# Attention and Fourier mixing on one core: late v chains and imaginary-row chains run as pairs on 64 rows each, with the score maxima in the same TensorE mode

## The chip, the cores and the metric

The kernel runs on one core of a Trainium2 chip. The metric is the device time of one execution in microseconds, the median of several runs; lower is better. Before the change it is 1739.28 us (three runs, 1739.17 to 1740.05).

## The reference, cut to what matters

```python
# S = 2048 rows, D = 512, H = 32 heads of 16
g = sigmoid((x * gate_w).sum(-1, keepdims=True))
# A: Fourier mixing, real part only
a = x @ dft_hid_re.T ;  b = x @ dft_hid_im.T
A = dft_seq_re @ a - dft_seq_im @ b
# B: softmax attention of all heads, scale 16 ** -0.5
q, k, v = split(x @ wqkv)
B = softmax(q @ k.T * scale) @ v @ wo
return g * A + (1 - g) * B
```

Everything is float32. The kernel keeps the precision by splitting an operand into a high and a low part (fp32r) and taking three products, high by high, high by low and low by high.

## The kernel before, in words

The work has three stages, one after the other on TensorE (PE).

**Stage 1** (lines 127 to 188) makes q and k from x and writes their high and low parts to DRAM.

**Stage 2** (lines 272 to 310) is the one that the change rewrites. It has 16 tiles of v (`for s in range(NT)`, line 272), then 16 tiles of imaginary rows b (line 296). A tile is a chain of 12 matmuls on all 128 rows of the array (four slices `kt` of 128 by three products, `mm3`, lines 78 to 81; rows here are those of the contraction) into one PSUM bank of pool `psS`. After the chain comes `visit` (line 260). From the eighth v tile on, until 44 units are made (`LEAD`), a visit makes two units ahead of time. A unit is a 128x512 block of scores for both heads of a pair: for each head one matmul on 48 rows (`a_tile`, line 217; head 0 in rows 0 to 47, head 1 in rows 64 to 111) and a DVE reduction that keeps only the row maxima (line 219). So 22 of the 32 visits hold four score matmuls each: three into pool `psA` (3 banks), the last into `psD` (1 bank). Behind the visit the chain's bank is emptied. A v tile takes an ACT copy and a DVE copy of half a bank (lines 280 and 281). A b tile takes `hi_lo` (line 74): an ACT cast to the high part, a DVE subtraction that waits for it, and a 512 KB store on SP's queue (line 305), through a buffer `hl` of which there are two. When a half of the 64 units of a pair is complete, `deferred` gets two steps (`m_parts`, `m_rows`) which reduce the maxima further and write them as rows behind q.

**Stage 3** (lines 770 to 824) holds the attention and the Fourier matmuls together. First come six pumps of real-row matmuls on 128 rows, then segments. A segment (line 744) follows a pattern of slots: `s` is a score matmul on 50 rows with an exponential on ACT behind it (lines 635 and 636), `a` a score matmul for a maximum, `|` the product of the exponentials with v (`pv`, line 644) for one unit. A slot of one letter also issues one matmul of a running chain, on 64 rows of the half of the array that the score does not use (line 349), so that the two stand side by side. Two segments make a pair of segments: in the second the chains move to the other half of the rows, and the scores too. At each such swap the first chain matmul waits for the last user (ACT or DVE) of the segment before (line 760), so that what the old half wrote into the chain's bank is there. Patterns: `THIN` with real-row chains of 12 (13 pairs of segments; each pair holds one whole chain, which its first segment begins), `FULL` with sequence chains of 48 (96 pairs, a chain begins in every third), `NINE` with projection chains of 9 (13 pairs).

PSUM has 8 banks: `psS` 3, `psA` 3, `psD` 1 and `acc` 1. The bank `acc` collects the `pv` products; it is filled with zeros once at the beginning (line 155), since the products write 17 of each 32 rows and all are copied out.

Of the kernel before, what the change touches and what calls it, by code (L numbers as in the profile page):

```python
# [9 lines left out]
F32 = mybir.dt.float32  # L10
# [5 lines left out]
P = 128  # L16
S = 2048
D = 512
# [13 lines left out]
def mix_kernel(ctx: ExitStack, tc: tile.TileContext, xa_t, xa, wqkv, w_hid, w_seq, wo, gate_w, out):  # L32
# [41 lines left out]
    def hi_lo(hi, lo, src, lo_eng=None):  # L74
        nc.scalar.copy(hi, src)  # L75
        (lo_eng or nc.vector).tensor_tensor(lo, src, hi.bitcast(F32), ALU.subtract)

    def mm3(ps, sh, sl, mh, ml, first, last):
        nc.tensor.matmul(ps, sh, mh, start=first, stop=False)  # L79
        nc.tensor.matmul(ps, sh, ml, start=False, stop=False)  # L80
        nc.tensor.matmul(ps, sl, mh, start=False, stop=last)  # L81
# [11 lines left out]
    def staged(src):  # L93
        raw = st1.tile([P, D], F32, name="raw", bufs=RAW)
        nc.sync.dma_start(raw, src)
        return raw
# [30 lines left out]
    with tc.tile_pool(name="qk", bufs=1, reuse_waits="tile") as pool:  # L127
        wh = pool.tile([P, 2, KT, D], F32R, name="wh")
        wl = pool.tile([P, 2, KT, D], F32R, name="wl")

        def mm_qk(ps, c, ct, tb, kt):
            cols = slice(ct * P, (ct + 1) * P)
            x = xab[tb][:, :, :, kt * P:(kt + 1) * P]
            mm3(ps, wh[:, c, kt, cols], wl[:, c, kt, cols], x[:, :, 0], x[:, :, 1], kt == 0, kt == KT - 1)

        def evac_qk(ps, c, ct, tb):
            hl = pool.tile([P, 2, D], F32R, name="hl", bufs=7)
            hi_lo(hl[:, 0], hl[:, 1], ps)
            nc.sync.dma_start(qk_d[c][:, ct * P:(ct + 1) * P, tb * 512:(tb + 1) * 512].rearrange("v p t -> p v t"),
                              hl.bitcast(F32))  # L140

        for kt in range(KT):
            add(wh[:, 0, kt], wl[:, 0, kt], wqkv[0, :, kt], nc.vector)
            add_x(0, kt)
        for kt in range(KT):
            add(wh[:, 1, kt], wl[:, 1, kt], wqkv[1, :, kt], nc.vector)
        for tb in range(1, 4):
            for kt in range(KT):
                add_x(tb, kt)
        for kt in range(KT):  # L150
            add(wv[0][kt], wv[1][kt], wqkv[2, :, kt], nc.gpsimd)
        for kt in range(KT):
            add(wch[:, kt], wcl[:, kt], w_hid[1, :, kt], nc.gpsimd)
        split(8)
        nc.vector.memset(acc, 0.0)

        xgs = {}

        def gate_row(s):

            xg = xgs.pop(s)
            nc.vector.scalar_tensor_tensor(xg, xg, 1.0, gwb, op0=ALU.mult, op1=ALU.mult, accum_out=z[:, s:s + 1])
            if s + 5 < NT:
                xgs[s + 5] = staged(xa[s + 5])

        for tb in range(4):
            if tb == 2:
                assert not todo and not loaded
                nc.sync.dma_start(gwb, gate_w.broadcast_to([P, D]))
                xgs.update({s: staged(xa[s]) for s in range(5)})  # L170
            for c in range(2):
                if tb == 0 and c == 0:
                    pss = [bank() for _ in range(4)]
                    for kt in range(KT):
                        for ct in range(4):
                            mm_qk(pss[ct], c, ct, tb, kt)
                    split(4)
                    for ct in range(4):
                        evac_qk(pss[ct], c, ct, tb)
                    continue  # L180
                for ct in range(4):
                    ps = bank()
                    for kt in range(KT):
                        mm_qk(ps, c, ct, tb, kt)
                    split(1 if ct % 2 and tb else 2)
                    evac_qk(ps, c, ct, tb)
                    if tb > 1:
                        gate_row(8 * (tb - 2) + 4 * c + ct)
# [22 lines left out]
    def a_tile(i, h, ps=None):  # L211
        p, j = divmod(i, 64)
        qt, kb = divmod(j, 4)
        if ps is None:
            ps = psA.tile([P, 512], F32, name="a")
        r = slice(64 * h, 64 * h + 48)
        nc.tensor.matmul(ps, qs[p % 2][r, qt * P:(qt + 1) * P], ks[p % 2][r, kb * 512:(kb + 1) * 512],  # L217
                         start=True, stop=True)
        user = nc.vector.tensor_reduce(mx[p % 2][:, h, qt, kb:kb + 1], ps, AX.X, ALU.max)  # L219
        hf = j // 32  # L220
        a_left[p, hf] = a_left.get((p, hf), 64) - 1
        if not a_left[p, hf]:
            deferred.extend((partial(m_parts, p, hf), partial(m_rows, p, hf)))
        return user
# [18 lines left out]
    def run_deferred():  # L243
        while deferred:
            deferred.pop(0)()


    ones = st1.tile([2, 2 * D], F32, name="hl", bufs=2)
    nc.gpsimd.memset(ones, 1.0)
    nc.gpsimd.memset(vt[:, :, :, 16:17], 1.0)  # L250
    for i in range(2):
# [5 lines left out]
    wrs = []  # L257
    a_next = 0

    def visit(i):  # L260

        nonlocal a_next
        if deferred:
            deferred.pop(0)()
        if i < 7 or a_next == LEAD:
            return
        for j in range(2):
            for h in range(2):
                a_tile(a_next, h, psD.tile([P, 512], F32, name="d") if j and h else None)
            a_next += 1  # L270

    for s in range(NT):
        t = xab[s // 4][:, s % 4]
        ps = psS.tile([P, 512], F32, name="s")
        for kt in range(KT):
            r = slice(kt * P, (kt + 1) * P)
            mm3(ps, t[:, 0, r], t[:, 1, r], wv[0][kt], wv[1][kt], kt == 0, kt == KT - 1)
        visit(s)
        pv = ps.rearrange("p (r h d) -> p r h d", h=2, d=DH)
        nc.scalar.copy(vt[:, s, :, 0:16], pv[:, :, 0])  # L280
        nc.vector.tensor_copy(vt[:, s, :, 17:33], pv[:, :, 1])
        if s in range(6, 14, 2):
            kt = (s - 6) // 2
            wt = st1.tile([P, 2, D], F32R, name="hl", bufs=2)
            hi_lo(wt[:, 0], wt[:, 1], wos.pop(0), nc.gpsimd)
            nc.sync.dma_start(wo_d[kt], wt.bitcast(F32))
            wrs.append(staged(w_hid[0, :, kt]))

    def spare(i, dt, name):

# [2 lines left out]

    wre = [[const.tile([P, D], F32R, name=f"wre{v}{kt}", tag=f"w{4 * v + kt}") for kt in range(KT)] for v in range(2)]
    ab = [xab[s // 4][:, s % 4] for s in range(NT)]
    for s in range(NT):
        t = ab[s]
        ps = psS.tile([P, 512], F32, name="s")
        for kt in range(KT):
            r = slice(kt * P, (kt + 1) * P)  # L300
            mm3(ps, t[:, 0, r], t[:, 1, r], wch[:, kt], wcl[:, kt], kt == 0, kt == KT - 1)
        visit(NT + s)
        bt = st1.tile([P, 2, D], F32R, name="hl", bufs=2)
        hi_lo(bt[:, 0], bt[:, 1], ps)
        nc.sync.dma_start(b_d[s], bt.bitcast(F32))
        if s < KT:
            hi_lo(wre[0][s], wre[1][s], wrs.pop(0), nc.gpsimd)
    run_deferred()
    assert a_next == LEAD
    right.__exit__(None, None, None)  # L310

# [139 lines left out]

    def inverse(hf, ct, n=4):
        rc = rcs.pop((hf, ct))
        for h in range(2):
            rows = rc[64 * h:64 * h + 16 * n]
            nc.vector.reciprocal(rows, rows)
            nc.sync.dma_start(r_d[hf][ct][h, :n].rearrange("p (c f) -> c p f", f=64), rows)

    def load_o(o, sm, hf, ct, q0, n=4):
# [205 lines left out]
    def issue(x, half, stop=True):  # L665
        chain, st, mv, after, last = x
        i = chain.mm(st, mv, half, last and stop)
        if stop and after:
            after()
        return i  # L670
# [73 lines left out]
    def segment(pattern, half, ds, stop):  # L744


        nonlocal users
        before, users = users, []
        ds = iter(ds)
        for slot in pattern.split():  # L750
            if slot == "|":
                values()
                continue
            if len(slot) == 1:
                x = next(ds, None)
                if x:
                    i = issue(x, half, stop)
                    users = []
                    if before:
                        tc.add_manual_dep(  # L760
                            i.ins, dict(before).get("s", before[0][1]).ins.name,
                            mybir.DependencyInfo(mybir.DependencyClass.Sync, mybir.DependencyReason.DATA))
                        before = None
            score(slot[0], 1 - half)
            if len(slot) == 2:
                score(slot[1].lower(), half)
        if deferred:
            deferred.pop(0)()
# [92 lines left out]
```

## Time and profile before

| | |
|---|---|
| median of 3 runs | 1739.28 us |
| profiled execution: its time, its span | 1738.59 us, 1736.8 us |
| granted TensorE clock, mean | 0.998 |
| stage 2: first maximum (line 217) to the first matmul of stage 3 (line 349) | 116.22 to 201.82 us |
| THIN segments | up to about 372 us |
| FULL segments | 374 to about 1516 us |
| NINE segments and the rest | from 1518 us |

The profile gives for each engine the busy time and for each group of instructions the count, the mean duration and what ended the idle time before it. In the timeline a row is a start, a duration, an engine and an operation; `PE` is a matmul, `PEld` a weight load. Matmuls are pipelined, so a row's duration is longer than the step from one matmul to the next: the steps are read from the starts. A PE that is shown as busy all the time can therefore still lose time between matmuls.

### The profile page before, as it was taken

The page shows a single profiled execution, that of the slowest core. Times are in us where ns is not written, and L with a number is a line of the kernel's source. Part 1 is how long each engine was busy: PE and PEld are TensorE (multiplying, and loading weights), DVE is VectorE, ACT ScalarE, POOL GpSimd, SP SyncE. Part 2 cuts the span into 40 slices and gives each one's busy share as a digit, 9 for nine tenths or more (in the row PEclk, how much of TensorE's full clock was granted, in tenths as well). Part 3 has the DMA queues.
Part 4 walks back from the last instruction along what each step waited for, and adds up shares of the span by engine and source line. Part 5 has one row for each costly group of instructions (what it writes and reads, how often), then busy time and mean ns, then how long its engine had stood idle before and what let it go on. Part 6 is the DMA issues. An engine that isn't in the chain of part 4 may idle for free.

```text
span 1736.8 us, 32902 instructions
## 1 busy us (share of the span) xinstructions
PE 1717.9 (99%) x12721; PEld 1036.8 (60%) x12721; DVE 1368.8 (79%) x2302; ACT 1153.1 (66%) x2257; POOL 447.3 (26%) x561
## 2 busy tenths in 40 slices
PE   8999999999999999999999999999999999999998
PEld 7876644456665666666566666666656666544443
DVE  5448688888888888888888888888888888899953
ACT  5211277776776677677677777767776776777776
POOL 1121122222232233222132343332333343200111
PEclk9999999999999999999999999999999999999999
DMA  9962500314141343414146435223142535460113
GB/s 293 337 153 109 158 2 8 56 31 80 38 87 44 74 113 83 77 44 74 43 90 240 94 105 108 68 64 71 49 82 67 124 93 98 166 153 23 38 28 128
DMA packets 82348, 164.79 MB, mean 95 GB/s; under 512 B 19712, under 2 KB 19968, under 8 KB 78352
## 3 DMA queue, kind: packets, MB, share of 16 engines
q1 hardware_dynamic: 77840, 162.30, 36.5%
q8 instruction: 100, 1.64, 0.4%
q0 software_dynamic: 4352, 0.39, 0.3%
q14 instruction: 56, 0.46, 0.1%
HBM read 107.47 MB, written 54.52 MB: 93 GB/s over the span
## 4 chain that ended last, share of the span: by engine, by line
PE 96%; ACT 2%; DVE 1%; DMA 0%; issue 0%; POOL 0%; DVEq 0%; SPq 0%; ACTq 0%; POOLq 0%
PE d L349 35%; PE acc L644 26%; PE s L635 12%; PE a L217 12%; PE s L79 3%; PE s L80 3%; PE s L81 3%; ACT pt L636 1%; PE a L79 1%; PE a L81 1%; PE a L80 1%; ACT y L365 0%; DVE mx L219 0%; PE a L349 0%; DMA qs<-mt 0%
## 5 line engine op out<-in xcount | busy, mean ns | idle before, releaser
L219 DVE TENSOR_REDUCE mx<-a 128x1 f32<-128x512 f32 x2026 | 1245.2, 683 | 251.3 <-PE a L217 233.0
L636 ACT ACTIVATE pt<-s 128x512 f32<-128x512 f32 x2008 | 1025.4, 620 | 391.8 <-PE s L635 333.2
L217 PE MATMUL a<-ks,qs 48*128 48x512 f32 x2026 | 811.9, 418 | 0.7 <-DVE mx L219 0.7
L635 PE MATMUL s<-qs,ks 50*128 50x512 f32 x2008 | 769.9, 413 | 1.3 <-DMA qs<-mt 0.9
L349 PE MATMUL d<-xab,ch 64*128 64x512 f32 x2016 | 648.4, 396 | 0.0
L644 PE MATMUL acc<-pt,vt 128*17 128x512 f32 x4096 | 500.3, 596 | 0.0
L349 PEld LDWEIGHTS d<-xab,ch 64*128 64x128 f32 x2016 | 366.1, 184 | 126.4 <-DVE mx L219 60.4
L635 PEld LDWEIGHTS s<-qs,ks 50*128 50x128 f32 x2008 | 365.7, 184 | 108.2 <-ACT pt L636 31.0
L217 PEld LDWEIGHTS a<-ks,qs 48*128 48x128 f32 x2026 | 365.9, 185 | 73.5 <-DVE mx L219 42.1
L349 PE MATMUL d<-xab,cl 64*128 64x512 f32 x1008 | 399.4, 396 | 0.0
L349 PEld LDWEIGHTS d<-xab,cl 64*128 64x128 f32 x1008 | 185.5, 184 | 65.2 <-DVE mx L219 40.8
L333 POOL CAST ch<-craw 128x512 fp32r<-128x512 f32 x126 | 77.4, 614 | 555.8 <-PE s L635 176.8
L644 PEld LDWEIGHTS acc<-pt,vt 128*17 128x17 f32 x4096 | 90.2, 96 | 205.8 <-issue 205.8
L334 POOL TENSOR_TENSOR cl<-craw,ch 128x512 fp32r<-128x512 f32 x126 | 162.5, 1290 | 10.2
L240 POOL DMA_DIRECT2D qs<-mt x128 | 72.2, 569 | 159.3 <-DVE mt L236 150.9
L349 PE MATMUL d<-wre,xab 64*128 64x512 f32 (+1 forms) x348 | 94.9, 405 | 2.6 <-ACT pt L636 2.5
L349 PEld LDWEIGHTS d<-wre,xab 64*128 64x128 f32 (+1 forms) x348 | 60.0, 185 | 39.3 <-issue 23.2
L349 PE MATMUL d<-wo_hl,o_hl 64*128 64x512 f32 (+1 forms) x261 | 70.8, 397 | 0.0
L75 ACT CAST hl<-s 128x512 fp32r<-128x512 f32 x32 | 18.8, 587 | 65.0 <-PE s L81 49.4
L349 PEld LDWEIGHTS d<-wo_hl,o_hl 64*128 64x128 f32 (+1 forms) x261 | 47.1, 185 | 16.2 <-issue 11.7
L231 POOL CAST nhl<-nm 128x16 fp32r<-128x16 f32 x32 | 6.3, 197 | 160.7 <-DVE nm L228 160.7
L366 POOL CAST xab<-y 128x512 fp32r<-128x512 f32 x16 | 9.8, 613 | 136.9 <-ACT y L365 108.9
(125 smaller groups left out, 932.7 us busy)
## 6 DMA issues: line engine op xcount, KB each, us to landing
craw<-w_seq SPq DMA_DIRECT2D x128, 256.0 KB
qk<-hl SPq DMA_DIRECT2D x32, 512.0 KB
qs<-qk SPq DMA_DIRECT2D x96, 128.0 KB
ks<-qk SPq DMA_DIRECT2D x96, 128.0 KB
b<-hl SPq DMA_DIRECT2D x16, 512.0 KB
xab<-b SPq DMA_DIRECT2D x16, 512.0 KB
o<-oe SPq DMA_DIRECT2D x62, 128.0 KB
oh<-nh SPq DMA_DIRECT2D x12, 512.0 KB
```

Source lines behind the costliest of these rows:

```text
L79: nc.tensor.matmul(ps, sh, mh, start=first, stop=False)
L80: nc.tensor.matmul(ps, sh, ml, start=False, stop=False)
L81: nc.tensor.matmul(ps, sl, mh, start=False, stop=last)
L217: nc.tensor.matmul(ps, qs[p % 2][r, qt * P:(qt + 1) * P], ks[p % 2][r, kb * 512:(kb + 1) * 512], start=True, stop=True)
L219: user = nc.vector.tensor_reduce(mx[p % 2][:, h, qt, kb:kb + 1], ps, AX.X, ALU.max)
L240: (nc.sync, nc.gpsimd)[h].dma_start(rows.rearrange("v (q b c) -> v b q c", q=8, b=4)[:, b], mt[hf][32 * b + h:32 * b + 32:2])
L333: nc.gpsimd.tensor_copy(h1, raw)
L334: nc.gpsimd.tensor_tensor(l1, raw, h1.bitcast(F32), ALU.subtract)
L349: i = nc.tensor.matmul(self.ps, st[r], mv[r], start=not self.begun, stop=stop)
L635: nc.tensor.matmul(ps, ks[p % 2][rr, kt * P:(kt + 1) * P], qs[p % 2][rr, q0:q0 + 512], start=True, stop=True)
L636: return nc.scalar.activation(pts[u][:, 2 * qb + h], ps, AF.Exp, bias=0.0, scale=DH ** -0.5)
L644: nc.tensor.matmul(acc[32 * j:32 * j + 17], vt[:, kt, p, 16 * h:16 * h + 17], pt[:, j], start=kt == 0, stop=kt == NT - 1)
```

## The change

The loops of stage 2 are written anew. The first eight v tiles stay as they were, without visits. The last eight v tiles and all 16 b tiles go in groups of four, each group as two pairs of tiles. A *phase* issues 12 steps for one pair: in each step one matmul of 64 rows for the first tile and one of the other 64 rows for the second. A group has four phases: pair 0 on one assignment of rows, pair 1 likewise, then pair 0 with the rows swapped, pair 1 swapped. So each chain has 24 half matmuls instead of 12 whole ones. A phase with maxima makes two units, one after step 3 and one after step 9 (phases 1 to 22 of 24); the last of the four scores uses the bank `acc` instead of `psD`, since every group has one chain in `psD` and three in `psS`. The first matmul of a swapped phase waits for the DVE reduction of head 1 of the first unit in the phase before. The banks of a pair are emptied after its second phase, both tiles behind one another. The filling of `acc` moves to the end of stage 2, and `hl` has four buffers instead of two.

In stage 3 two things change. `inverse` takes the reciprocal of both heads' sums in one instruction where all four pairs are there (7 of 8 calls). And a segment whose first chain matmul begins a new chain no longer waits for the segment before.

The diff, cut to its core:

```diff
-        nc.vector.memset(acc, 0.0)
-    ones = st1.tile([2, 2 * D], F32, name="hl", bufs=2)
+    ones = st1.tile([2, 2 * D], F32, name="hl", bufs=4)
-    def visit(i):
-        nonlocal a_next
-        if deferred:
-            deferred.pop(0)()
-        if i < 7 or a_next == LEAD:
-            return
-        for j in range(2):
-            for h in range(2):
-                a_tile(a_next, h, psD.tile([P, 512], F32, name="d") if j and h else None)
-            a_next += 1
+    def x_mm(s, wh, wl):
+        t = xab[s // 4][:, s % 4]
+        for kt in range(KT):
+            h1, l1 = (t[:, v, kt * P:(kt + 1) * P] for v in range(2))
+            yield from ((h1, wh[kt]), (h1, wl[kt]), (l1, wh[kt]))
...
+    made, user = 0, None
+    def phase(pair, half, maxima):
+        nonlocal a_next, user
+        before, user = user, None
+        for j in range(12):
+            for x, (ps, ops, done) in enumerate(pair):
+                st, mv = ops[j]
+                r = slice(64 * (half ^ x), 64 * (half ^ x) + 64)
+                i = nc.tensor.matmul(ps, st[r], mv[r], start=not half and not j, stop=half == 1 and j == 11)
+                if not j and not x and half:
+                    tc.add_manual_dep(i.ins, before.ins.name,
+                                      mybir.DependencyInfo(mybir.DependencyClass.Sync, mybir.DependencyReason.DATA))
+            if maxima and j in (3, 9):
+                for h in range(2):
+                    used = a_tile(a_next, h, acc if h and j == 9 else None)
+                user = user or used
+                a_next += 1
+        if half:
+            for ps, ops, done in pair:
+                done(ps)
+        if deferred:
+            deferred.pop(0)()
+    def pairs_of(tiles, wh, wl, done):
+        nonlocal made
+        tiles = list(tiles)
+        for i in range(0, len(tiles), 4):
+            new = []
+            for s in tiles[i:i + 4]:
+                ps = psD.tile([P, 512], F32, name="d") if s % 4 == 1 else psS.tile([P, 512], F32, name="s")
+                new.append((ps, list(x_mm(s, wh, wl)), partial(done, s)))
+            for half in range(2):
+                for pair in (new[:2], new[2:]):
+                    phase(pair, half, 0 < made and a_next < LEAD)
+                    made += 1
+    for s in range(8):
...
+    pairs_of(range(8, NT), *wv, v_done)
...
+    pairs_of(range(NT), *([w[:, kt] for kt in range(KT)] for w in (wch, wcl)), b_done)
     run_deferred()
+    nc.vector.memset(acc, 0.0)
...
         rc = rcs.pop((hf, ct))
+        if n == 4:
+            nc.vector.reciprocal(rc, rc)
         for h in range(2):
             rows = rc[64 * h:64 * h + 16 * n]
-            nc.vector.reciprocal(rows, rows)
+            if n < 4:
+                nc.vector.reciprocal(rows, rows)
...
                 if x:
+                    before = before if x[0].begun else None
                     i = issue(x, half, stop)
```

`v_done` and `b_done` hold what stood behind the visit before: the two copies of a v tile (with a split of `wo` at tiles 6, 8, 10 and 12), and for a b tile the cast, the subtraction and the store, at the first four b tiles also the split of a slice of the real weights (`wre`, a cast on ACT and a subtraction on POOL).

More of the change, by code (lines that the diff above doesn't have):

```diff
@@ L258, in mix_kernel, with v_done @@
     a_next = 0
-    def visit(i):
-        nonlocal a_next
-        if deferred:
-            deferred.pop(0)()
-        if i < 7 or a_next == LEAD:
-            return
-        for j in range(2):
-            for h in range(2):
-                a_tile(a_next, h, psD.tile([P, 512], F32, name="d") if j and h else None)
-            a_next += 1
-    for s in range(NT):
+    def x_mm(s, wh, wl):
         t = xab[s // 4][:, s % 4]
-        ps = psS.tile([P, 512], F32, name="s")
         for kt in range(KT):
-            r = slice(kt * P, (kt + 1) * P)
-            mm3(ps, t[:, 0, r], t[:, 1, r], wv[0][kt], wv[1][kt], kt == 0, kt == KT - 1)
-        visit(s)
+            h1, l1 = (t[:, v, kt * P:(kt + 1) * P] for v in range(2))
+            yield from ((h1, wh[kt]), (h1, wl[kt]), (l1, wh[kt]))
+    def v_done(s, ps):
         pv = ps.rearrange("p (r h d) -> p r h d", h=2, d=DH)
@@ L283, in mix_kernel @@
             kt = (s - 6) // 2
-            wt = st1.tile([P, 2, D], F32R, name="hl", bufs=2)
+            wt = st1.tile([P, 2, D], F32R, name="hl", bufs=4)
             hi_lo(wt[:, 0], wt[:, 1], wos.pop(0), nc.gpsimd)
@@ L287, in mix_kernel, with b_done @@
             wrs.append(staged(w_hid[0, :, kt]))
+    def b_done(s, ps):
+        bt = st1.tile([P, 2, D], F32R, name="hl", bufs=4)
+        hi_lo(bt[:, 0], bt[:, 1], ps)
+        nc.sync.dma_start(b_d[s], bt.bitcast(F32))
+        if s < KT:
+            hi_lo(wre[0][s], wre[1][s], wrs.pop(0), nc.gpsimd)
+    made, user = 0, None
[33 more added lines that the diff above has]
+    for s in range(8):
+        ps = psS.tile([P, 512], F32, name="s")
+        ops = list(x_mm(s, *wv))
+        for i, (st, mv) in enumerate(ops):
+            nc.tensor.matmul(ps, st, mv, start=not i, stop=i == len(ops) - 1)
+        v_done(s, ps)
+    pairs_of(range(8, NT), *wv, v_done)
     def spare(i, dt, name):
@@ L295, in mix_kernel @@
     ab = [xab[s // 4][:, s % 4] for s in range(NT)]
[L296 to L307, printed above, removed]
+    pairs_of(range(NT), *([w[:, kt] for kt in range(KT)] for w in (wch, wcl)), b_done)
     run_deferred()
+    nc.vector.memset(acc, 0.0)
     assert a_next == LEAD
```

## The prediction

> **What bounds the kernel now.** I read the page first: busy time and the chain of work that ended last.
>
> ```profile
> span 1736.8 us, 32902 instructions
> ...
> PE 1717.9 (99%) x12721; PEld 1036.8 (60%) x12721; DVE 1368.8 (79%) x2302; ACT 1153.1 (66%) x2257; POOL 447.3 (26%) x561
> ...
> PE 96%; ACT 2%; DVE 1%; DMA 0%; issue 0%; POOL 0%; DVEq 0%; SPq 0%; ACTq 0%; POOLq 0%
> ```
>
> PE is the bound: 96% of the chain is PE, and every step that PE loses in stage 2 or 3 moves the end. So the question is where PE steps further than its matmuls need. I read that from the starts in the timeline, since PE shows no idle time there. First one visit of a b tile:
>
> ```profile
> 148.45 0.40 PE L81 MATMUL s<-wch,xab 128*128 128x512 f32 x1
> ...
> 148.78 0.73 PE L217 MATMUL a<-ks,qs 48*128 48x512 f32 x3
> ...
> 149.12 0.39 PE L217 MATMUL d<-ks,qs 48*128 48x512 f32 x1
> 149.32 1.89 DVE L219 TENSOR_REDUCE mx<-a 128x1 f32<-128x512 f32 x3 [0.84 <-PE a L217]
> ...
> 149.44 0.50 PE L79 MATMUL s<-wch,xab 128*128 128x512 f32 x1
> ...
> 149.79 0.39 PE L80 MATMUL s<-wcl,xab 128*128 128x512 f32 x1
> ...
> 151.12 0.68 DVE L219 TENSOR_REDUCE mx<-d 128x1 f32<-128x512 f32 x1
> ...
> 151.72 0.68 DVE L76 TENSOR_TENSOR hl<-s,hl 128x512 fp32r<-128x512 f32 x1
> ...
> 152.11 0.40 PE L81 MATMUL s<-wch,xab 128*128 128x512 f32 x1
> ...
> 152.43 0.73 PE L217 MATMUL a<-ks,qs 48*128 48x512 f32 x3
> ...
> 152.97 1.89 DVE L219 TENSOR_REDUCE mx<-a 128x1 f32<-128x512 f32 x3 [0.57 <-PE a L217]
> ```
>
> From 149.79 to 152.11 lie ten steps of 128-row matmuls: 0.232 us each. From the last of one chain (148.45) to that of the next (152.11) is 3.66 us. Twelve chain matmuls and two pairs of scores (head 0 and head 1 stand side by side, 48 rows each) are 14 steps, 3.25 us. The other 0.41 us is two gaps. The last score (149.12) belongs to the second pair, so the first pair started at 148.89, where 148.68 was due: 0.21. The next chain matmul was due at 149.35, and its follower at 149.79 puts it at 149.56: 0.21 again. Each is a change between 128 rows and 64 rows. A visit of a v tile shows the same:
>
> ```profile
> 141.52 0.73 PE L217 MATMUL a<-ks,qs 48*128 48x512 f32 x3
> ...
> 142.52 0.39 PE L80 MATMUL s<-wv,xab 128*128 128x512 f32 x1
> ...
> 144.45 0.41 DVE L281 COPY vt<-s 128x256 f32<-128x256 f32 x1
> ...
> 144.81 0.39 PE L81 MATMUL s<-wv,xab 128*128 128x512 f32 x1
> ...
> 145.13 0.73 PE L217 MATMUL a<-ks,qs 48*128 48x512 f32 x3
> ```
>
> The period is 3.61 us (141.52 to 145.13), ten steps take 2.29 (142.52 to 144.81), and 3.61 less 14 steps of 0.229 leaves 0.40.
>
> DVE has room, but little: the three reductions from 149.32 and the fourth at 151.12 step by 0.60, the subtraction comes 0.60 behind, and 0.57 us of 3.66 is idle. That matters below.
>
> **The change, part by part.**
>
> *Phases in place of visits.* Before: 9 v visits and 13 b visits with maxima, 9 x 0.40 + 13 x 0.41 = 8.9 us lost at 44 mode changes. After: all is on 64 rows from the ninth v tile on; two changes stay, one into stage 2's phases, one out into stage 3's first pump, 0.4 us. That removes **8.5 us**, if two half chains side by side step as fast as one whole chain. Their work is 288 pairs of half matmuls for 288 matmuls before, and the maxima are 44 pairs in both. No row of before has two chains side by side; the nearest is a chain beside scores in stage 3:
>
> ```profile
> 600.95 0.39 PE L349 MATMUL d<-xab,cl 64*128 64x512 f32 x1
> 600.95 0.39 PE L635 MATMUL s<-qs,ks 50*128 50x512 f32 x1
> 601.18 0.39 PE L349 MATMUL d<-xab,ch 64*128 64x512 f32 x1
> ...
> 604.16 0.39 PE L349 MATMUL d<-xab,ch 64*128 64x512 f32 x1
> ```
>
> Chain and score start together, and from 600.95 to 604.16 the chain takes 14 steps of 0.229. So I take 0.231 for a pair, between 0.229 and 0.232: an uncertainty of 332 x 0.0025, 0.8 us each way. Where a swapped phase puts the rows in the other order, a score for head 0 follows a chain matmul on the same rows; both columns of rows still get one matmul per step, so I count nothing.
>
> *Waits at the swaps.* New are 12 waits of PE (every swapped phase: 4 in v, 8 in b) for the second reduction of the phase before. Behind the waiting matmul stands all of PE. Is that reduction done in time? A phase is 14 x 0.231 = 3.23 us. A score pair after step 3 starts at 0.92, and 152.97 lies 0.43 after the score at 152.54 that it follows (152.43 and 0.11 for the weights), so reduction 1 can start at 1.35, and 3 at 2.97. The second half of DVE's load comes in lumps: after a swapped phase, two tiles are emptied at once.
>
> ```profile
> 148.93 0.59 ACT L75 CAST hl<-s 128x512 fp32r<-128x512 f32 x1 [3.31 <-PE s L81]
> ...
> 149.41 0.62 ACT L75 CAST wre<-raw 128x512 fp32r<-128x512 f32 x1
> ```
>
> The cast starts 0.48 after the last matmul's start (148.45), so 0.25 into the next phase; the next ACT operation follows after 0.48. Subtractions behind each other step like these of stage 1:
>
> ```profile
> 17.67 0.69 DVE L76 TENSOR_TENSOR hl<-a,hl 128x512 fp32r<-128x512 f32 x1
> 18.35 0.69 DVE L76 TENSOR_TENSOR hl<-s,hl 128x512 fp32r<-128x512 f32 x1
> ```
>
> That is 0.68. Now b, group after group. In phase 3 (pair 0's tiles being emptied) DVE comes free at 0.94, subtracts until 2.30, and reduces until 2.90, 3.50, 4.10 and 4.70. In phase 0 of the next group that is 1.47: subtractions to 2.83, reductions to 3.43, 4.03, 4.63, 5.23. In phase 1: 2.00, reductions to 2.60 and **3.20**, 4.40 the last. The swap at 3.23 waits for just that 3.20, and a signal and a weight load come on top: a stall of about 0.15 us. Phase 2 then has its second reduction at 2.55, in time, and its fourth at 4.17, which is 0.94 in phase 3: the circle closes. Three b groups have that swap with such a load before it. The first is worse: between its casts stand casts of `wre` (149.41 above), the second subtraction ends at 2.53 in place of 2.30, and all comes 0.23 later: a score waits some 0.2, the swap some 0.15. Together 0.35 + 2 x 0.15, about **0.7 us** lost. In v a copy takes 0.41 (row 144.45) for 0.68, and nothing binds. Bounds: nothing, or a whole reduction at each of the 12 waits, 12 x 0.60 = 7.2.
>
> *PSUM.* The score banks: three in `psA` and `acc`, each used once per phase, and a bank is asked for again 3.23 us later; in the table above its reduction ended before, but for the one case counted. A pair's chain banks are free at 2.30 or 2.83 of a phase, asked for at 3.23. The `hl` buffers:
>
> ```profile
> 199.66 0.59 ACT L75 CAST hl<-s 128x512 fp32r<-128x512 f32 x1 [2.65 <-DMA b<-hl]
> ```
>
> With two buffers the last casts wait for their stores as soon as chains come at less than 3.66 us. With four, a store has a whole group (13 us), so a burst of two tiles costs nothing; SP has the same number of stores. If the cover fails, ACT's wait of 2.65 appears once or twice.
>
> *No wait at a fresh chain.* In stage 3 I looked for first chain matmuls that wait. In THIN:
>
> ```profile
> PEld d L349 <- ACT pt L636: 6.3, 12, 0.5
> ```
>
> Twelve times, of 13 pairs of segments: those that begin a chain. One of them:
>
> ```profile
> 300.79 0.58 ACT L365 COPY y<-d 128x512 f32<-128x512 f32 x1
> ...
> 301.71 0.50 PE L217 MATMUL a<-ks,qs 48*128 48x512 f32 x1
> ...
> 302.42 0.49 PE L349 MATMUL d<-wre,xab 64*128 64x512 f32 x1 [0.21 <-ACT pt L636]
> ...
> 303.67 0.40 PE L217 MATMUL a<-ks,qs 48*128 48x512 f32 x1
> ...
> 307.89 0.50 PE L217 MATMUL a<-ks,qs 48*128 48x512 f32 x1
> ...
> 313.71 0.50 PE L217 MATMUL a<-ks,qs 48*128 48x512 f32 x1
> ```
>
> The pair of scores starts at 301.71 (0.11 for weights, so 301.82), the chain was due at 302.05 and comes 0.47 later, since the exponential that it waits for stands in ACT's queue behind the copy `y`. From a view of ACT alone:
>
> ```profile
> 301.26 1.10 ACT L636 ACTIVATE pt<-s 128x512 f32<-128x512 f32 x2
> ```
>
> The second of these ends at 302.36; that is the one. This segment takes 6.18 us (to 307.89), the other of the pair 5.82 (to 313.71): 0.36 is the most that goes. What is late next: the second `s` slot needs a score bank that the same exponential empties. Chain and first `s` go at 302.05, the second chain matmul at 302.28, the second `s` still at 302.53 and the four slots behind it one step each, so the last `a` starts at 303.45 in place of 303.67. I take 0.22, 12 x 0.22 = **2.6 us**; bounds 0 and 12 x 0.36 = 4.3. In FULL and NINE all waits of chain matmuls look alike:
>
> ```profile
> PEld d L349 <- DVE mx L219: 102.1, 120, 0.9
> ...
> PEld d L349 <- issue: 52.1, 66, 0.9
> ```
>
> The longest is 0.9 whether DVE or nothing is named: the 128-row `pv` and its mode change, not the wait. There I count nothing.
>
> *The rest at nothing.*
>
> ```profile
> L456 DVE RECIPROCAL rc<-rc 64x64 f32<-64x64 f32 (+1 forms) x16 | 8.5, 531 | 2.8 <-DMA rc<-o 2.5
> ...
> L155 DVE MEMSET acc<- 128x512 f32 x1 | 0.5, 485 | 0.1
> ```
>
> Half the reciprocals (0.53 each) leave DVE, which isn't on the chain. The zeros of `acc` leave a DVE that is waiting for loads, and come after the last subtractions: the first maxima of stage 3 are reduced about 1 us later, `psA`'s third bank covers it, and without that cover it is 1 us once. Instructions of `deferred`, their DMAs on SP and POOL, and the stores keep their order; the maxima rows are issued some 17 us before stage 3 needs them.
>
> **Sum.** 8.5 - 0.7 + 2.6 = 10.4 us. The profiled execution, 1738.59 (span 1736.8 and 1.8 around it), becomes 1728.2. It lies 0.7 below the median of before, so the median becomes **1728.9**.
>
> **The rivals.**
>
> 1. *DVE becomes the bound.* A b group needs 16 x 0.60 + 4 x 0.68 = 12.3 us of DVE in 12.9. If in each phase DVE idles 0.57 as it does in each visit now, because a subtraction waits for its cast while scores wait behind it, a group takes 14.6, 3.65 per phase, and b gains nothing; v, at 4 x 2.4 + 4 x 0.41 + 2.3 = 13.5 per group, 3.38 per phase, gains some 2. With THIN: 1739.3 - 4.6 = 1734.7. For it: the lumps of two. Against it: in the table DVE always has something waiting. The Trainium skill, "TensorEngine Tiling (Array Packing)", PSUM Bottleneck, states that packing speeds TensorE but not the emptying of PSUM; by it this rival would be the likeliest, but the idle 0.57 per visit shows DVE still below PE. Chance 0.13.
>
> 2. *The fresh chain's wait hides another*: THIN gains nothing, and 1731.5 is left. For it: ACT's queue is dense there. Against it: the other segment of each pair has no such gap. Chance 0.10.
>
> 3. *Slower: two chains do not stand side by side as chain and score do.* If the second's matmul holds the first up, each of the 288 pairs costs more; from 0.231 + 10.4 / 288 = 0.267 us on, the change loses. The worst by a row is that a pair takes a matmul's whole 0.39 us: 288 x 0.16 = 46, less 10.4, so 1775. For it: both matmuls of a pair have 64 rows and run sums, and the order of rows flips at the maxima. Against it: the 0.229 above. The Trainium skill, "TensorE: Matmul & The Clock Gate", Measured speedup vs the span model, gives 3.07 times for four row tiles, not 4. By that as an estimate a pair would take 0.231 x 4 / 3.07 = 0.30 and the time come to 1749; stage 3's rows don't agree with it. Chance 0.07.
>
> **How the numbers follow.** The forecast, with 0.70, is 1728.9. The low end takes the best of each bound, 8.5 + 0.8 + 4.3 = 13.6: 1725.5. The high end takes in rivals 1 and 2: 1735. Beyond it lie rival 3 and little else. About 0.2% (3.5 us) is what a measurement can tell from no change; faster by more than that means below 1735.8: the forecast and rivals 1 and 2 but for a slice, 0.90; within it 0.03; slower 0.07.
>
> **What would show it.** Right: in stage 2 chain matmuls in two rows with one start, 0.23 apart; no gaps of 0.2 around line 217; some 77 us from the ninth v tile to stage 3's first pump; the 12 waits of THIN's chain matmuls gone and its two segments nearly alike. Wrong: a step above 0.25 in the phases (rival 3), or the first matmul of swapped phases waiting for DVE by half a microsecond each time (rival 1), or ACT waiting for stores of b.

## The result and the profile after

The kernel after takes **1727.97 us** (median of 4 runs, 1727.72 to 1728.15) beside 1739.22 us for the kernel before on the same chip (4 runs, 1739.16 to 1740.05). The ratio is 0.9935, with a 95% interval of 0.9923 to 0.9947: 0.65% faster. The prediction was 1728.9 us, in a range from 1725.5 to 1735.

The profiled execution of after took 1727.72 us. Its page shows the same bound as before:

```profile
span 1725.9 us, 33460 instructions
...
PE 1711.7 (99%) x13009; PEld 1049.2 (61%) x13009; DVE 1364.2 (79%) x2295; ACT 1150.7 (67%) x2257; POOL 447.3 (26%) x561
...
PE 98%; ACT 1%; DVE 0%; DMA 0%; issue 0%; DVEq 0%; ACTq 0%
```

There are 288 matmuls more, since each of the 24 chains that run in pairs has 24 half matmuls in place of 12 whole ones, and yet the span is 10.9 us shorter. As before, what was lost shows in the starts, not in PE's busy share. Line numbers in the rows are those of after: L216 is the score for a maximum, L218 its reduction, L295 the chain matmul of a phase, L327 that of the first eight v tiles, L381 the chain of stage 3, L670 and L671 score and exponential, L679 `pv`.

First PE's timeline of after at the two borders of the paired part of stage 2 and in one phase of b (start, duration, operation; x2 is two matmuls in one row):

```profile
95.70 0.39 PE L327 MATMUL s<-wv,xab 128*128 128x512 f32 x1
...
116.78 0.84 PE L327 MATMUL s<-wv,xab 128*128 128x512 f32 x3
117.55 0.49 PE L295 MATMUL s<-wv,xab 64*128 64x512 f32 x1
117.56 0.50 PE L295 MATMUL d<-wv,xab 64*128 64x512 f32 x1
117.89 0.39 PE L295 MATMUL s<-wv,xab 64*128 64x512 f32 x1
...
118.12 0.39 PE L295 MATMUL s<-wv,xab 64*128 64x512 f32 x1
...
149.79 0.39 PE L295 MATMUL s<-wcl,xab 64*128 64x512 f32 x1
149.81 0.39 PE L295 MATMUL d<-wcl,xab 64*128 64x512 f32 x1
...
152.13 0.40 PE L216 MATMUL acc<-ks,qs 48*128 48x512 f32 x1
152.14 0.40 PE L216 MATMUL a<-ks,qs 48*128 48x512 f32 x1
...
194.66 0.48 PE L295 MATMUL s<-wch,xab 64*128 64x512 f32 x2
195.07 0.74 PE L381 MATMUL d<-wre,xab 128*128 128x512 f32 x2
```

The reader sees what the change is: two chains with one start, in the banks `s` and `d`, and the two heads' scores (152.13 and 152.14) in the same rhythm. From 149.79 to 152.13 are ten steps, 0.234 us each; the pair of scores at 152.13 follows in the same step, and no gap of 0.2 stands before it. A change of mode is left at 117.55 (0.34 to the follower at 117.89) and one at 195.07. Between these two lie 77.5 us, where the prediction had said some 77.

Where the time came from, by stretches of the two profiled executions. The rows of before:

```profile
94.37 0.39 PE L79 MATMUL s<-wv,xab 128*128 128x512 f32 x1
...
201.82 0.85 PE L349 MATMUL d<-wre,xab 128*128 128x512 f32 x3
...
374.51 0.47 PE L349 MATMUL d<-xab,chl 64*128 64x512 f32 x1 [0.73 <-ACT pt L636]
...
1496.65 0.47 PE L635 MATMUL s<-qs,ks 50*128 50x512 f32 x1 [0.91 <-DMA qs<-mt]
```

and of after, first THIN's two segments (the starts of their score pairs and the first chain matmul), then the entry to FULL:

```profile
293.97 0.49 PE L216 MATMUL a<-ks,qs 48*128 48x512 f32 x1
...
294.30 0.63 PE L381 MATMUL d<-wre,xab 64*128 64x512 f32 x2
...
299.96 0.50 PE L216 MATMUL a<-ks,qs 48*128 48x512 f32 x1
...
305.79 0.50 PE L216 MATMUL a<-ks,qs 48*128 48x512 f32 x1
...
364.80 0.49 PE L381 MATMUL d<-xab,chl 64*128 64x512 f32 x1
```

| stretch | before | after | gained |
|---|---|---|---|
| start to the first v matmul | 94.37 | 95.70 | -1.33 |
| first v matmul to the second matmul of stage 3's first pump (0.23 after 201.82, 0.34 after 195.07) | 107.68 | 99.71 | 7.97 |
| from there through THIN to the first FULL matmul | 172.46 | 169.39 | 3.07 |
| FULL, NINE and the end | 1362.3 | 1361.1 | 1.2 |
| span | 1736.8 | 1725.9 | 10.9 |

The first row is a difference between executions (the last section), and 0.91 of the fourth is the wait at 1496.65 of before, for a transfer; in after no row names such a wait there. So the change itself is worth 7.97 in stage 2, 3.07 from the pumps through THIN to the entry to FULL, and about 0.3 behind it.

### The profile page after: what moved, and what is told of

Same layout as the page of the kernel before. It is cut to its first block, busy times and chain, and to the rows that moved or that the text cites. A ratio compares the mean times of both kernels' runs of the same rounds, so it can differ in the third digit from the quotient of the medians.

```text
span 1725.9 us, 33460 instructions
## 1 busy us (share of the span) xinstructions
PE 1711.7 (99%) x13009; PEld 1049.2 (61%) x13009; DVE 1364.2 (79%) x2295; ACT 1150.7 (67%) x2257; POOL 447.3 (26%) x561
## 4 chain that ended last, share of the span: by engine, by line
PE 98%; ACT 1%; DVE 0%; DMA 0%; issue 0%; DVEq 0%; ACTq 0%
PE d L381 35%; PE acc L679 28%; PE a L216 12%; PE s L670 12%; PE s L295 3%; PE s L327 1%; PE d L295 1%; PE s L79 1%; PE s L80 1%; PE a L79 1%; PE a L80 1%; PE s L81 1%; PE a L81 1%; ACT pt L671 0%; PE a L381 0%; PE acc L216 0%
## 5 line engine op out<-in xcount | busy, mean ns | idle before, releaser
L218 DVE TENSOR_REDUCE mx<-a 128x1 f32<-128x512 f32 x2026 | 1245.8, 682 | 243.6 <-PE a L216 227.6
L671 ACT ACTIVATE pt<-s 128x512 f32<-128x512 f32 x2008 | 1024.2, 620 | 389.1 <-PE s L670 328.9
L216 PE MATMUL a<-ks,qs 48*128 48x512 f32 x2026 | 813.9, 416 | 0.7 <-DVE mx L218 0.7
L670 PE MATMUL s<-qs,ks 50*128 50x512 f32 x2008 | 769.7, 413 | 0.4 <-ACT pt L671 0.2
L381 PE MATMUL d<-xab,ch 64*128 64x512 f32 x2016 | 648.5, 396 | 0.0
L679 PE MATMUL acc<-pt,vt 128*17 128x512 f32 x4096 | 500.7, 596 | 0.0
L381 PEld LDWEIGHTS d<-xab,ch 64*128 64x128 f32 x2016 | 366.0, 184 | 126.0 <-DVE mx L218 60.4
L670 PEld LDWEIGHTS s<-qs,ks 50*128 50x128 f32 x2008 | 366.1, 184 | 110.0 <-ACT pt L671 32.4
L216 PEld LDWEIGHTS a<-ks,qs 48*128 48x128 f32 x2026 | 368.2, 185 | 67.3 <-DVE mx L218 40.6
L381 PE MATMUL d<-xab,cl 64*128 64x512 f32 x1008 | 399.4, 396 | 0.0
L381 PEld LDWEIGHTS d<-xab,cl 64*128 64x128 f32 x1008 | 185.5, 184 | 64.9 <-DVE mx L218 40.8
L679 PEld LDWEIGHTS acc<-pt,vt 128*17 128x17 f32 x4096 | 90.6, 96 | 205.9 <-issue 205.8
L381 PE MATMUL d<-wre,xab 64*128 64x512 f32 (+1 forms) x348 | 93.8, 402 | 0.1
L381 PEld LDWEIGHTS d<-wre,xab 64*128 64x128 f32 (+1 forms) x348 | 60.0, 185 | 32.3 <-issue 23.6
L381 PE MATMUL d<-wo_hl,o_hl 64*128 64x512 f32 (+1 forms) x261 | 71.0, 397 | 0.0
L381 PEld LDWEIGHTS d<-wo_hl,o_hl 64*128 64x128 f32 (+1 forms) x261 | 47.2, 185 | 16.1 <-issue 11.7
```

The lines of the kernel that those rows point to most:

```text
L381: i = nc.tensor.matmul(self.ps, st[r], mv[r], start=not self.begun, stop=stop)
L670: nc.tensor.matmul(ps, ks[p % 2][rr, kt * P:(kt + 1) * P], qs[p % 2][rr, q0:q0 + 512], start=True, stop=True)
L671: return nc.scalar.activation(pts[u][:, 2 * qb + h], ps, AF.Exp, bias=0.0, scale=DH ** -0.5)
L679: nc.tensor.matmul(acc[32 * j:32 * j + 17], vt[:, kt, p, 16 * h:16 * h + 17], pt[:, j], start=kt == 0, stop=kt == NT - 1)
```

## The experiments

Eight kernels were run, each beside the kernel before on the same chip. Ratios are to the kernel before (1738.84 to 1739.19 us in these runs). "Stage 2" below is the second row of the table above, "THIN" the third (pumps and entry to FULL included), and "FULL" goes from the first FULL matmul to the `pv` that begins at 1487.94 in after, which ends the 189th of its 192 segments. A *fresh* segment is one that begins a chain; behind the entry FULL has 31 of them in this stretch.

**Before, with only the fresh chain's wait dropped** (`e1`). The theory was that THIN's gain and stage 2's are independent; the rival, that the wait hides another one.

```diff
                 if x:
+                    before = before if x[0].begun else None
                     i = issue(x, half, stop)
```

> The kernel before with one line of the change: a segment whose first chain matmul begins a new chain does not wait. My theory: 12 swaps of THIN gain 0.19 us each and the entry into FULL 0.77, as the two traces show, so 3.1 us in all: 1736.1. Rival 2 of the prediction (the wait hides another, and the gain seen in the THIN segments comes from the new stage 2 ahead of them): 1739.2. In the profile: none of the 12 waits of chain matmuls for ACT in THIN; stage 2 as before.

Measured: 1736.44 us (11 runs, 1735.95 to 1737.5), ratio 0.9984 (0.9975 to 0.9993). That is 2.7 less than the kernel before beside it (1739.12). The 12 waits of THIN's chain matmuls for `pt` are gone. With before's stage 2 (107.71), THIN takes 169.42, 3.04 less than in before: the gain stands alone and is the expected one there, so the rival is out. The median gained 0.4 less than the expected 3.1; in the trace FULL's fresh segments take 0.67 more than in before, which `e2` and `e7` explain below.

**After, with that wait kept** (`e2`): the line of the diff above is taken out of the kernel after.

> The changed kernel with the wait of fresh chains put back: the new stage 2 alone. My theory: 1728.0 + 3.1 = 1731.1, so that the two parts add up. Rival (stage 2 is worth all of it): 1728.0. In the profile: stage 2 as short as in the changed kernel, from the first v matmul to the first pump about 99.5 us, and the 12 waits in THIN back.

Measured: 1729.31 us (5 runs, 1728.6 to 1730.35), ratio 0.9941 (0.9929 to 0.9953), between the two expectations. Its waits in THIN, of the weight loads and of the matmuls (in total, times, longest):

```profile
PEld d L381 <- ACT pt L671: 6.3, 12, 0.5
...
PE d L381 <- ACT pt L671: 3.3, 13, 0.7
```

The waits are back (the thirteenth of the second row is the entry to FULL), and THIN is 3.03 us longer than in after. But the median rose by 1.3 only. Stage 2 is the same (99.72), so something in the rest has become shorter: FULL takes 1.0 less than in after (1122.17 against 1123.14), and 0.7 of this lies in the fresh segments; what is left between this sum and the 1.3 is no more than executions differ by. The prediction had counted FULL's waits at nothing. Here the sign is against the change: in FULL the dropped wait seems to cost. `e7` was made to test that alone.

**Only b in pairs** (`e3`): v as sixteen whole chains with eight visits, b as in after.

```diff
-    for s in range(8):
+    for s in range(NT):
...
+        visit(s)
         v_done(s, ps)
-    pairs_of(range(8, NT), *wv, v_done)
```

> The changed kernel with the 16 v tiles as whole chains on 128 rows and a visit behind each of the last eight (8 visits, 16 units, 16 more mode changes), and pairs only for b (28 units in phases 1 to 14 of 16). My theory, 0.2 us per mode change: 8 x 0.40 = 3.2 us more than the changed kernel: 1731.2. Rival (the gain comes from the longer stretch between the emptying of banks, not from the modes; then v with its light copies hardly counts): within 1 us of the changed kernel, 1728 to 1729. In the profile: gaps of 0.2 us on both sides of the visits' maxima, none in the phases of b.

Measured: 1734.09 us (1732.43 to 1735.56), ratio 0.9968 (0.9956 to 0.9981): slower than either expected. The timeline shows why:

```profile
146.77 0.68 DVE L218 TENSOR_REDUCE mx<-d 128x1 f32<-128x512 f32 x1
147.50 0.18 PEld L295 LDWEIGHTS d<-wch,xab 64*128 64x128 f32 x1 [2.55 <-DVE mx L218]
147.50 0.50 PE L295 MATMUL d<-wch,xab 64*128 64x512 f32 x1 [2.11 <-DVE mx L218]
```

The last visit's fourth score lies in the bank `d`, the first pair of b asks for it at once, and PE waits 2.11 us for the reduction. That is of the variant's own making; the kernel after avoids it by giving the fourth score the bank `acc`.

**The same with the fourth score in `acc`** (`e8`).

```diff
-                a_tile(a_next, h, psD.tile([P, 512], F32, name="d") if j and h else None)
+                a_tile(a_next, h, acc if j and h else None)
```

> The variant with v as whole chains with eight visits and only b in pairs, but with the visits' fourth score in the bank acc, so that the first pair of b finds the bank in psD free. Theory: the 2.11 us wait of the first pair goes, and stage 2 (first v matmul to the second matmul of the first pump) takes 99.7 + 8 x 0.39 = 102.8 us against 104.9 before it; the time is 1727.97 + 3.1 = 1731.1 us, with up to 1 us between executions. What v's pairs bring by themselves is then these 3.1. Rival: the wait stands for DVE's load at the change from v to b, not for the bank; it moves to another matmul, and stage 2 stays at about 104.9 and the time at 1733 to 1734.

Measured: 1731.69 us (1730.6 to 1734.17), ratio 0.9962 (0.9949 to 0.9974). The wait is gone, and stage 2 is down from `e3`'s 104.93 to 102.43 (L338 and L392 are here what L327 and L381 are in after):

```profile
95.57 0.39 PE L338 MATMUL s<-wv,xab 128*128 128x512 f32 x1
...
197.66 0.73 PE L392 MATMUL d<-wre,xab 128*128 128x512 f32 x2
```

So the rival, that DVE's load makes the wait, is out. So is the rival of `e3`, that the modes don't count and v with its light copies hardly gains: v's pairs alone bring 2.72. The 8.0 us of stage 2 split into 5.25 (before to `e8`) and 2.72 (`e8` to after). Counted in mode changes, before has 44, `e8` 16 (eight into visits, seven out of them, since the last leads straight into the phases, and one into stage 3), after 2. The second part is 14 changes, 0.194 each. The first is 28 changes, which by the prediction's 0.2 would be 5.6; the 0.35 that is missing is about what b's step costs: up to 0.234 for a pair where before's whole chains step 0.232, with 192 pairs of chain matmuls and 28 of scores at most 0.44. The expected 3.1 had overlooked that the last visit has no second change.

**After, with the small parts as before** (`e4`): zeros of `acc` at the beginning too, reciprocals per head.

```diff
+        nc.vector.memset(acc, 0.0)
...
-        if n == 4:
-            nc.vector.reciprocal(rc, rc)
...
-            if n < 4:
-                nc.vector.reciprocal(rows, rows)
+            nc.vector.reciprocal(rows, rows)
```

> The changed kernel with the two small parts undone: acc is also filled with zeros at the beginning, and the reciprocals are taken head by head as before. My theory: both lie off the path, 1728.0 within 0.5. Rival: the first matmul of the changed kernel's trace starts 0.4 us later and its first v matmul 1.3 us later than before; if the missing fill or what it does to the order at the beginning causes that, this kernel has its first v matmul at 94.4 us like the kernel before, not at 95.7, and takes 1726.7.

Measured: 1728.51 us (1727.29 to 1728.83), ratio 0.9934 (0.9921 to 0.9948). The time alone can't tell this kernel from after. The traces can. Six segments of FULL hold the reciprocals of four pairs. Each of these six takes 6.02 to 6.05 us in the three kernels with one reciprocal per head (before, `e1`, `e4`), and 5.94 to 5.96 in the seven with one for both, like the segments around it. So the merged reciprocals are worth about 0.5 us, where the prediction had nothing. One of the six in `e4`, and the same in after:

```profile
571.81 1.08 DVE L489 RECIPROCAL rc<-rc 64x64 f32<-64x64 f32 x2
572.92 0.69 DVE L219 TENSOR_REDUCE mx<-a 128x1 f32<-128x512 f32 x1
```

```profile
572.61 0.51 DVE L487 RECIPROCAL rc<-rc 128x64 f32<-128x64 f32 x1
573.64 0.69 DVE L218 TENSOR_REDUCE mx<-a 128x1 f32<-128x512 f32 x1 [0.52 <-PE a L216]
```

Behind the single reciprocal DVE waits 0.52 us for PE; behind the two it goes on without a pause.

The zeros cost nothing at either place: from the first v matmul to the first FULL matmul `e4` takes what after takes (99.73 and 169.38). Its first v matmul starts at 94.84, neither at 94.4 nor at 95.7, and `e2`, without zeros at the beginning, starts at 94.47: the zeros are not what moves the start.

**A swap that waits for the last maximum** (`e5`): the first matmul of a swapped phase waits for the fourth reduction of the phase before instead of the second.

```diff
-                user = user or used
+                user = used
```

> The changed kernel, but a swapped phase waits for the fourth reduction of the phase before instead of the second. My theory by the prediction's table: the fourth ends about 0.94 to 1.2 us after the phase's end, and a signal and a weight load come on top, so each of the 12 swaps stalls 1.1 to 1.3 us: 13.5 us more, 1741.5. Rival (PE is far from DVE there, the choice of the reduction is a matter of order only): less than 3 us more, below 1731. In the profile: the first chain matmul of each swapped phase waits for DVE, 12 times.

Measured: 1741.66 us (10 runs, 1740.28 to 1744.62), ratio 1.0014 (1.0004 to 1.0023): slower than the kernel before. PE's waits between 117 and 210 us, and one of the rows:

```profile
PE s L295 <- DVE mx L218: 11.0, 12, 0.9
```

```profile
137.81 0.63 PE L295 MATMUL s<-wv,xab 64*128 64x512 f32 x4
139.35 0.50 PE L295 MATMUL s<-wv,xab 64*128 64x512 f32 x1 [0.92 <-DVE mx L218]
...
139.69 0.39 PE L295 MATMUL s<-wv,xab 64*128 64x512 f32 x1
```

Twelve swaps, twelve waits of about 0.92, and stage 2 is 14.2 us longer: 1.18 per swap. In the rows, the last of the four matmuls from 137.81 starts at 138.05 (137.81 + 0.63 - 0.39), its follower was due at 138.28 and starts at 139.35, 1.07 late, and the next step takes 0.34 for 0.23. One line of the schedule decides over more than the whole gain. The kernel after has the same twelve waits for an earlier reduction, and they cost next to nothing, because that one is done in time. This is the point that the prediction's table of DVE times was made for.

**Two buffers `hl` instead of four** (`e6`).

```diff
-    ones = st1.tile([2, 2 * D], F32, name="hl", bufs=4)
+    ones = st1.tile([2, 2 * D], F32, name="hl", bufs=2)
```

(and likewise at the two other places of that name)

> The changed kernel with two buffers hl instead of four. My theory: a group empties two tiles in each of two phases behind one another, a store of 512 KB lands about 3.3 us after its subtraction, so the second two casts of each b group wait 1.5 us or more for stores; DVE stands behind them in order, and the chain banks of pair 1, the scores and the swaps come late: some 2 us per b group, 5 to 9 us more, 1733 to 1737. Rival (the stores' wait is hidden by PE's own time, as in the kernel before, where two casts waited and PE did not): 1728.0. In the profile: ACT waits for stores of b in the middle of stage 2, and PE for DVE.

Measured: 1732.55 us (1731.84 to 1734.03), ratio 0.9962 (0.9948 to 0.9976), a little under the expected range. ACT's wait, in the waits of `e6` from 117 to 205 us:

```profile
ACT hl L75 <- DMA b<-hl: 9.5, 4, 3.1
```

Before had two such waits, both for its last two tiles (2.65 and 1.98), and PE's steps show no gap there; here are four, of up to 3.1, and they do reach PE: stage 2 is 2.86 longer and the first pumps with THIN 1.8. In after ACT has no wait for `DMA b<-hl` at all between 117 and 196 us. The four buffers are a working part of the change, not a precaution.

**The wait kept in FULL alone** (`e7`): dropped where an exponential is among the users of the segment before, that is in THIN, at the entry to FULL and in NINE; kept for FULL's fresh chains.

```diff
-                    before = before if x[0].begun else None
+                    before = before if x[0].begun or "s" not in dict(before) else None
```

> The kernel after, but in FULL a segment that begins a chain waits again for the segment before; only in THIN, at the entry to FULL and in NINE, where an exponential is among the users, the wait stays away. Theory: in FULL the wait is worth something, since without it a fresh segment's chain and scores step 0.234 us instead of 0.230 for the first half; 31 fresh segments are 0.024 us longer each (5.970 against 5.946), together 0.75 us. Then the time is 1727.97 - 0.75 = 1727.2 us, the fresh segments of FULL are back at 5.95, and THIN stays at 163.0 from the first pv to the first FULL segment. Rival: the 0.75 is a difference between executions and not of the wait; then the fresh segments keep 5.97 and the time stays 1728.0, or they go back and the loss appears at the next segment.

Measured: **1726.23 us** (5 runs, 1726.12 to 1727.33), ratio 0.993 (0.9916 to 0.9943). The kernel before took 1738.84 beside it. This is the best version that was run: 12.6 less than before, where after was 11.25 less beside its own. The interval overlaps with that of after, so for the size the trace speaks. Of after, a fresh segment of FULL, from `pv` to `pv`, five steps of its chain, and the `pv` at which the stretch "FULL" ends:

```profile
541.50 1.91 PE L679 MATMUL acc<-pt,vt 128*17 128x512 f32 x16
...
543.68 0.40 PE L381 MATMUL d<-xab,ch 64*128 64x512 f32 x1
...
544.85 0.39 PE L381 MATMUL d<-xab,ch 64*128 64x512 f32 x1
...
547.48 1.91 PE L679 MATMUL acc<-pt,vt 128*17 128x512 f32 x16
...
1487.94 1.91 PE L679 MATMUL acc<-pt,vt 128*17 128x512 f32 x16
```

The same of `e7`:

```profile
540.47 1.91 PE L679 MATMUL acc<-pt,vt 128*17 128x512 f32 x16
...
542.65 0.39 PE L381 MATMUL d<-xab,ch 64*128 64x512 f32 x1
...
543.81 0.39 PE L381 MATMUL d<-xab,ch 64*128 64x512 f32 x1
...
546.42 1.91 PE L679 MATMUL acc<-pt,vt 128*17 128x512 f32 x16
...
1486.39 1.91 PE L679 MATMUL acc<-pt,vt 128*17 128x512 f32 x16
```

The segment takes 5.98 without the wait and 5.95 with it. Five steps of its chain take 1.17 without (543.68 to 544.85, 0.234 each) and 1.16 with it (542.65 to 543.81, 0.232 each). Over FULL, `e7` takes 1122.55 (363.84 to 1486.39) for 1123.14 in after: 0.59 less, near the expected 0.75. The fresh segments alone are 0.68 shorter, the others together 0.1 longer. The same holds in all ten traces: the 31 together take 184.4 us in the three kernels with the wait (before, `e2`, `e7`) and 185.0 to 185.2 in the seven without. The rest of the distance to after in the profile is mostly the start (94.74 for 95.70 to the first v matmul), which the last section takes up. That the wait's absence costs some 0.02 us per fresh segment is shown; why PE then steps a little wider is not. What is seen is only that the order in which the weight loads of chain and score begin is another one.

## Why the prediction was right, point by point

*Phases in place of visits, 8.5.* Right. The 42 changes measured 0.19 to 0.20 each. The pair's step was 0.23 in v (117.89 to 118.12) and in b 0.234 in the first group of tiles (149.79 to 152.13), 0.232 in the last: b began just beyond the 0.2335 that had been allowed.

*Waits at the swaps, 0.7.* The place was right in part, the size too large: of the three swaps named, two are late in the starts, by 0.06 and 0.04 (first steps of 0.29 and 0.27), the third is not. The 0.15 that the prediction set for each was not worked out from rows. The waits of after between 117 and 196 us, and the busy times from 144 to 183 (PE, PEld, DVE, ACT, POOL):

```profile
DVE mx L218 <- PE a L216: 8.0, 17, 2.9
...
PEld s L295 <- DVE mx L218: 0.2, 1, 0.2
```

```profile
144.00:183.00 39.00, 39.00 (x336) 34.28 (x334) 36.02 (x63) 7.92 (x15) 7.87 (x10) 1.00 0.36 136
```

One wait for a reduction is left to see, 0.2 us at a weight load. DVE is busy 92% in b and PE all the time. The two terms together, 8.5 less 0.7, gave 7.8; measured were 7.97. The wider step and the smaller stalls cancel, so the sum is better than its parts, by luck.

*No wait at a fresh chain, 2.6.* Right in mechanism, short by one wait. In the rows of after the chain (294.30) follows its score pair (293.97) by 0.33, where before it was 0.71 (301.71 to 302.42); the fresh segment takes 5.99 (293.97 to 299.96) in place of 6.18, the other 5.83. Over the twelve that is 2.30, 0.19 each where the prediction took 0.22. The rest, 0.77, is a thirteenth wait that the prediction didn't see: the entry to FULL, at 374.51 in before (0.73 for `pt`), begins a chain too. In the view of the weight loads it had stood under a wait for POOL, and only PE's own row names the exponential.

*FULL's fresh chains at nothing.* This step failed, by a small size: the prediction read that all waits there look alike, at 0.9, and concluded that dropping one changes nothing. The waits do look alike, but the segment behind is 0.02 us longer without it, 31 times: some 0.7 lost (`e1`, `e2`, `e7`).

*The rest at nothing.* The zeros yes (`e4`), and with four buffers no cast of b waits for a store. The reciprocals no: 0.5 gained (`e4`). The step that failed is "DVE, which isn't on the chain": in the segments with the reciprocals DVE's room of 0.52 us is used up by the second one, and the segment becomes longer.

That these two misses have opposite signs, and so leave little behind THIN (about 0.3 was gained there), is luck. The median lies 0.9 below the forecast, about the size of the thirteenth wait. By its own terms, the low end of the range comes to 1725.7 and not 1725.5; nothing hangs on it.

*The rivals.* Rival 1, DVE as the bound: out, since a phase of b with maxima takes 3.25 to 3.32 us where the rival had 3.65; DVE has 8% left. The Trainium skill, "TensorEngine Tiling (Array Packing)", PSUM Bottleneck, says that packing does not speed the emptying of PSUM. Here PE is not held back so, at DVE's 92%; but in `e5`, where a swap waits for two reductions more, the loss was 14 us. Rival 2, a second wait behind the fresh chain's: out by `e1`, whose THIN gains 3.04. Rival 3, two chains that hold each other up: out by the step of 0.234. The Trainium skill, "TensorE: Matmul & The Clock Gate", Measured speedup vs the span model, would have given 0.30 as an estimate; for two tiles of 64 rows the trace does not agree.

## What to carry to other kernels

Read PE's loss from the starts of its matmuls, and count the changes between 128 and 64 rows: at the 0.2 us each that they cost here, putting neighbouring work into one mode is worth as much as it has such changes, if the emptying engine still fits into the shorter period. Which of several reductions a swap waits for decides the rest, so write out the slower engine's times phase by phase before choosing it. And look at a dropped wait stage by stage: the same line gained 3.07 us in one stage and lost 0.7 in the next, and the best version keeps it where it helps.

## What the runs showed of the hardware

The start of the program differs between executions: the first v matmul began between 94.37 and 95.70 us in the ten traces, and between 94.47 and 95.70 in the seven whose code is the same up to there. Much of it is how long TensorE steps slowly at first. Before, and after:

```profile
8.41 0.63 PE L79 MATMUL s<-xab,wh 128*128 128x512 f32 x1
8.84 0.46 PE L80 MATMUL s<-xab,wh 128*128 128x512 f32 x1
9.13 0.40 PE L81 MATMUL s<-xab,wl 128*128 128x512 f32 x1
```

```profile
10.94 0.58 PE L81 MATMUL a<-xab,wl 128*128 128x512 f32 x1
11.36 0.39 PE L79 MATMUL s<-xab,wh 128*128 128x512 f32 x1
11.59 0.40 PE L80 MATMUL s<-xab,wh 128*128 128x512 f32 x1
```

The steps are 0.43 until 8.84 in the one and until 11.36 in the other, and soon 0.23 from then on: ten steps of 0.43 in place of five. The granted clock reads 1.00 in the slow stretch of both profiles, so these rows don't name the cause. The Trainium skill, "TensorE: Matmul & The Clock Gate", Part 1: The HAM clock gate, says that the slow stretch lasts some 3.4 us and varies with where a free-running window stands. The trace agrees that it varies; it lasted about 3.5 us in the one and 5.6 in the other, from the first matmuls at 5.38 and 5.78, so the second is longer than the page's figure. One late score of FULL is the other thing that varies: in before it waits 0.91 for a transfer (1496.65), in `e3` 1.31, in `e5` 1.19, in `e8` 0.20, and in after no row shows a wait. Both together are some 2 us between two profiles, more than twice the smaller terms of this sum, which is why those terms were read from stretches and not from whole times.

A weight load's wait can hide a matmul's own: the entry to FULL showed as a wait for POOL at the weights (1.62, at 374.48 in before) and as one for ACT at the matmul (0.73). The two have to be read side by side.
